# Output chunks in shared double buffers and the first keys in two transfers, in a top-32 attention with two MLPs

## The chip, the cores and the metric

The kernel runs on one core of a Trainium2 chip. The metric is the device time of one execution in microseconds (us). A core has five engines that run side by side and wait for each other by semaphores: TensorE (PE, matmuls; PEld is its weight load), VectorE (DVE), ScalarE (ACT), GpSimd (POOL) and SyncE (SP, which here only issues DMA transfers). Each engine takes its instructions strictly in order, so an instruction that waits holds up everything behind it on its engine. ACT also issues DMAs here: those of the output.

## The reference

Attention keeps the 32 largest scores of each row; then two MLPs follow, on 2304 tokens with model width 512 and hidden width 2048.

```python
scores = scale * np.matmul(q, k.transpose(0, 1, 3, 2))          # 4 batches, 8 heads, 576 x 576, head width 64
kth = np.partition(scores, -top_k, axis=-1)[..., -top_k:-top_k + 1]   # top_k = 32
scores = np.where(scores >= kth, scores, -1000000000.0)
attn = softmax(scores)                                          # written out in the reference
x = (attn @ v) reordered to [2304, 512]
h = np.maximum(x @ w_in, 0.0);   x = h * h @ w_out              # first MLP
h = x @ w_in2;   out = np.maximum(0.01 * h, h) @ w_out2         # second MLP
```

## The kernel before

**Tiling.** Tokens are cut into units (`UNITS`: a batch, a first row, 64 to 320 rows), and each unit has four head pairs. A unit and head pair gives score tiles of 128 rows; two tiles make a pair, and 72 pairs run one after the other through the whole attention. For each pair DVE finds the 32 largest of each row in four rounds of MAX8 (L867) with MATCH_REPLACE8 between them (L869). ACT turns the scores into exponentials (L321, L325), PE transposes them (L339, L354) and multiplies them with the values (L425 for the first two units, L436 later). The scores themselves are PE matmuls (L303) that ACT copies out of PSUM (L304).

**Split numbers.** Products are made of a rounded high part and a low part. `load_k` (L228) fetches the keys of a head pair, both heads in one transfer into `kraw`; `split_k` makes the high part (L128 on ACT for the first two key loads, L130 on POOL later) and the low part (L265; on DVE for the first load, on POOL later). `load_q` (L272) and `split_q` (L282) do the same for queries. For the first unit (256 rows, two heads) the first pair of tiles needs head 0 alone, the second pair head 1.

**MLPs.** When the tokens of a block (`BLOCKS`: 512, 256, 384, 512, 256, 384) are ready, generator `moe` runs its two layers, 16 steps of the hidden width each: matmuls into `h` (L619), ACT's `ga` and `gh` (L629, L630; L636, L638 in the second layer), the low part `gl` (L639), and matmuls into the accumulators `acc` (L656 in layer 0, L658 in layer 1). In the first block each step also converts its weights from 64-bit to 32-bit pieces (`w_convert`: `wraw` in, working buffer `wc`, L532 to L553) and stores them; later blocks load them back (`w_load`).

**Output.** At the end of layer 1 a block has n/128 accumulators. For each, L674 copies 512 columns out of PSUM into `y`, and L676 sends it to DRAM from ACT's queue, in two pieces where a chunk spans two units. `y` is the first half of a tile of 1024 columns with the tag `wc`, of which there are two buffers (`WCB = 2`); these are the buffers of the weight conversion. So the third chunk of a block waits until the transfer of the first has landed.

**What sets the order.** Work is put into numbered slots (`at`): 16 slots to a pair. `z` is the slot of a unit's first scores; keys are asked for at `z - 62`, queries at `z - 70` where nothing earlier holds them back. Instructions are emitted slot by slot, and a scheduler then lays out each engine's queue by priority and by its own model of the times, so that a small edit can shift rows all along the queues.

Of the kernel before, what the change touches and what calls it, by code (L numbers as in the profile page):

```python
# [8 lines left out]
F = mybir.dt.float32  # L9
# [49 lines left out]
WCB = 2  # L59
# [27 lines left out]
def topk_attention_moe_moe2_kernel(  # L87
# [12 lines left out]
    P = 128  # L100
# [8 lines left out]
    PE, ACT, DVE, POOL, SP = nc.tensor, nc.scalar, nc.vector, nc.gpsimd, nc.sync  # L109

    const = ctx.enter_context(tc.tile_pool(name="const", bufs=1))
    pool = ctx.enter_context(tc.tile_pool(name="work", bufs=2))
# [27 lines left out]
    for u in units:  # L140
        for hp in range(NHP):
            n = u["n"]
            uh = dict(u=u, hp=hp, n=n, b=u["b"], first=(u["t0"] == 0), i0=u["i"], ti=len(tiles), idx=len(uhs),
                      c0=P * (hp % 2) if n == 64 else 0)
# [14 lines left out]
    def direct(uh):  # L159
        return uh["b"] not in EARLY  # L160

    def kept(uh):
        return uh["u"]["i"] == KEPT

    def score_slot(ti):
        return 16 * (ti // 2) - DLEAD + 5 * (ti % 2)
# [10 lines left out]
    def split(uh):  # L177
        return uh["u"]["i"] >= NATIVE
# [36 lines left out]
    def at(slot, fn, *a):  # L215
        events.setdefault(slot, []).append((fn, a))
# [4 lines left out]
    def load_k(b, hp, st):  # L221
        if b in EARLY:
            KT[b, hp] = ahead.tile([P, 2, S], R, tag="KTa", name="KTa", bufs=KPB)
        else:
            KT[b, hp] = pool.tile([P, 2, S], R, tag="KT", name="KT", bufs=4)
        x = ahead if b in EARLY else pool
        st["k"] = x.tile([P, 2, S], F, tag="kraw", name="kraw", bufs=1 if b in EARLY else KRB)
        SP.dma_start(st["k"], k[b, hp])  # L228

    VT = {}  # L230
    vdram = {}
# [349 lines left out]
    def rows(g0, n):  # L581

        got = []
        for u in units:
            a, e = max(g0, u["g0"]), min(g0 + n, u["g0"] + u["n"])
            if a < e:
                got.append((a - g0, e - a, u["b"] * S + u["t0"] + a - u["g0"]))
        return got

    def moe(j, layer):  # L590
# [6 lines left out]
        for f in range(NF + LAG):  # L597
            conv = iter(())
            if f < NF:
# [24 lines left out]
                h = two.pop(0)  # L624
# [41 lines left out]
        for c in range(na):  # L666
            if layer == 0:
                xh, xl = x[c]
                with tc.high_priority(offset=SEAM):
                    ACT.activation(xh[:, 0:n], acc[c][:, 0:n], AF.Copy)  # L670
                    DVE.tensor_tensor(xl[:, 0:n], acc[c][:, 0:n], xh.bitcast(F)[:, 0:n], op=OP.subtract)
            else:
                y = pool.tile([P, 1024], F, tag="wc", name="y", bufs=WCB)[:, 0:512]
                ACT.activation(y, acc[c], AF.Copy)  # L674
                for p0, n0, r0 in rows(blk["g0"] + c * P, P):
                    ACT.dma_start(out[r0:r0 + n0, :], y[p0:p0 + n0])  # L676
# [9 lines left out]
    def after(z, *keys):  # L686
        return max([z] + [used[k] + 1 for k in keys if k in used])

    order = []
    for uh in in_time + [uh for uh in uhs if not direct(uh)]:  # L690
        b, hp, i = uh["b"], uh["hp"], uh.get("di")
        z = uh["zs"]
        if uh["first"] and direct(uh):
            st = {"i": i}
            st["n"] = len(order)
            order.append(b)
            z0 = after(z - 62, ("kraw", st["n"] - KRB), *[("KT", x, hp) for x in range(b)])
            at(z0, load_k, b, hp, st)
            for h in range(2):
                at(z0 + 12 * h + 11, split_k, b, hp, st, h)  # L700
            used["kraw", st["n"]] = z0 + 23
            assert z0 + 24 <= z
        if (b, hp) not in vdone or split(uh) and VTB < NHP:
            vdone.add((b, hp))
            zv = score_slot(uh["ti"]) + DLEAD + 4
            if split(uh):
                zv = max(zv, opened)
            at(zv, load_v, uh)
            if split(uh):
                at(zv + 6, split_v, uh, 0)  # L710
                at(zv + 9, split_v, uh, 1)
        if not direct(uh):
            continue
        uh["qs"] = qsets[i % 2]
        z0 = after(z - 70, ("qraw", i - 2))
        z1 = max(after(z - 20, ("q", i - 2)), z0 + 6)
        assert z1 + 4 <= z
        at(z0, load_q, uh)
        at(z1, split_q, uh, 0)
        at(z1 + 4, split_q, uh, 1)  # L720
        used["qraw", i] = z1 + 4
        used["q", i] = used["KT", b, hp] = (z if kept(uh) else score_slot(uh["last"])) + 2
# [129 lines left out]
    while slot <= last:  # L852
        p, i = divmod(slot, 16)
# [89 lines left out]
```

## Time and profile before

| What | us |
|---|---|
| Median of three runs (1192.93, 1192.21, 1192.61) | 1192.61 |
| The profiled execution: its own time | 1189.77 |
| Its span, from the first to the last instruction | 1188.0 |
| Busy in it: PE | 1124.0 |
| DVE | 872.1 |
| ACT | 820.1 |
| POOL | 744.8 |

The profile is of one execution, whose time is 2.84 us below the median; 1.77 us of it lie outside the span. Busy time of an engine says which engine has the least room over the whole span, and not which one sets the end in a given stage: for that the busy time in short stretches is read, then what an engine waited for there, then the chain of work that ended last. The granted clock (PEclk) is a share of TensorE's full rate: 1.00 is 2.4 GHz and 0.50 is 1.2 GHz.

### The profile page before, as it was taken

The numbers are of one execution on the slowest core, as the hardware profiler recorded it, in microseconds if no ns is written. First come the engines' busy times: TensorE is split into PE (matmuls) and PEld (weight loads), VectorE is DVE, ScalarE is ACT, GpSimd is POOL, SyncE is SP. The second block draws the span as 40 slices with busy tenths as digits, with TensorE's granted clock in tenths as the row PEclk, the third lists the DMA queues.
The fourth block names the chain that finished last, engine by engine and source line by source line (L and its number), as shares of the span: only waits on it lengthen the run. The fifth ranks groups of instructions, "written<-read, shape, count | busy, mean of one in ns | idle before, by whom it ended". The sixth has DMA issues, their size and how long they took to land.

```text
span 1188.0 us, 20096 instructions
## 1 busy us (share of the span) xinstructions
PE 1124.0 (95%) x6376; PEld 985.5 (83%) x6376; DVE 872.1 (73%) x1828; ACT 820.1 (69%) x1823; POOL 744.8 (63%) x958
## 2 busy tenths in 40 slices
PE   5899977989899999999999999999999999999997
PEld 4777765868688899898998998788888899998996
DVE  7999999888886668999999999989997400110010
ACT  6999998899989667887676777556766743332322
POOL 7968846999879677677886775767665653002100
PEclk9999989999899999999999999999999999999999
DMA  9868756899999698799888888667776499779973
GB/s 307 287 216 276 264 187 230 312 334 333 394 353 360 199 336 293 240 346 371 312 264 296 286 283 287 217 219 219 232 234 215 151 326 334 256 252 351 346 258 119
DMA packets 108201, 329.53 MB, mean 277 GB/s; under 512 B 17216, under 2 KB 25408, under 8 KB 104000
## 3 DMA queue, kind: packets, MB, share of 16 engines
q1 hardware_dynamic: 105472, 323.53, 79.8%
q10 hardware_dynamic: 2624, 4.72, 1.1%
q8 instruction: 52, 0.85, 0.3%
q14 instruction: 53, 0.43, 0.1%
HBM read 257.03 MB, written 71.17 MB: 276 GB/s over the span
## 4 chain that ended last, share of the span: by engine, by line
PE 57%; DVE 21%; ACT 12%; DMA 5%; issue 2%; POOL 2%; ACTq 0%; SPq 0%; POOLq 0%; DVEq 0%
PE h L619 22%; PE acc L658 13%; DVE m L867 10%; PE acc L656 9%; DVE w L869 8%; PE att L425 3%; PE att L436 3%; PE att L339 3%; ACT e L321 2%; ACT stage L304 1%; PE sp L303 1%; ACT e L325 1%; DMA wraw<-in_w_dram 1%; DMA out_dram<-y 1%; ACT s L304 1%
## 5 line engine op out<-in xcount | busy, mean ns | idle before, releaser
L619 PE MATMUL h<-xh,wi 128*128 128x512 f32 (+2 forms) x1280 | 345.9, 344 | 9.7 <-ACT ga L629 4.5
L867 DVE MAX8 m<-w 128x8 f32<-128x576 f32 x432 | 315.1, 756 | 1.8
L619 PEld LDWEIGHTS h<-xh,wi 128*128 128x128 f32 x1280 | 225.4, 190 | 38.6 <-ACT ga L629 6.7
L639 POOL TENSOR_TENSOR gl<-ga,gh 128x512 fp32r<-128x512 f32 (+2 forms) x160 | 162.5, 1018 | 137.2 <-ACT gh L638 110.9
L869 DVE MATCH_REPLACE8 w<-m,w 128x576 f32<-128x576 f32 x288 | 215.2, 751 | 0.5
L619 PE MATMUL h<-xl,wi 128*128 128x512 f32 (+2 forms) x640 | 203.3, 338 | 0.0
L347 POOL TENSOR_TENSOR PTs<-whole,PTs 128x512 fp32r<-128x512 f32 x112 | 144.6, 1297 | 43.7 <-ACT whole L346 43.2
L656 PE MATMUL acc<-gh,wo 128*128 128x512 f32 (+2 forms) x768 | 156.5, 343 | 0.8 <-ACT y L674 0.5
L658 PE MATMUL acc<-wo,gh 128*128 128x512 f32 x576 | 152.1, 396 | 0.5 <-ACT gh L638 0.5
L656 PEld LDWEIGHTS acc<-gh,wo 128*128 128x128 f32 x768 | 127.4, 190 | 13.4 <-ACT y L674 0.7
L321 ACT ACTIVATE e<-s,m 128x576 f32<-128x576 f32 x144 | 112.9, 785 | 32.3 <-DVE m L867 27.4
L639 DVE TENSOR_TENSOR gl<-ga,gh 128x384 fp32r<-128x384 f32 x32 | 17.9, 559 | 152.1 <-ACT gh L638 149.4
L619 PEld LDWEIGHTS h<-xl,wi 128*128 128x128 f32 x640 | 120.0, 189 | 10.6
L636 ACT ACTIVATE ga<-h 128x512 f32<-128x512 f32 (+2 forms) x96 | 46.6, 491 | 116.3 <-PE h L619 114.8
L658 PEld LDWEIGHTS acc<-wo,gh 128*128 128x128 f32 x576 | 105.4, 188 | 21.2 <-ACT gh L638 0.9
L867 DVE MAX8 m<-s 128x8 f32<-128x576 f32 x144 | 104.3, 754 | 17.7 <-ACT s L304 15.2
L325 ACT ACTIVATE e<-e,nb 128x576 f32<-128x576 f32 x144 | 111.5, 782 | 1.8 <-POOL nb L315 1.7
L869 DVE MATCH_REPLACE8 w<-m,s 128x576 f32<-128x576 f32 x144 | 108.2, 752 | 0.6
L339 PE MATMUL att<-ident,e 128*128 128x128 f32 x576 | 90.1, 277 | 7.6 <-DVE wc L548 3.0
L334 POOL TENSOR_SCALAR e<-e,rc 128x576 f32<-128x576 f32 x112 | 82.5, 748 | 16.0 <-DVE rc L330 14.5
L656 PE MATMUL acc<-gl,wo 128*128 128x512 f32 (+2 forms) x384 | 88.3, 349 | 3.8 <-POOL gl L639 3.8
L631 POOL TENSOR_TENSOR ga<-ga 128x512 f32<-128x512 f32 (+2 forms) x80 | 66.3, 829 | 36.9 <-ACT gh L630 36.7
(90 smaller groups left out, 2117.4 us busy)
## 6 DMA issues: line engine op xcount, KB each, us to landing
wi<-wd SPq DMA_DIRECT2D x160, 512.0 KB, 5.1
wo<-wd SPq DMA_DIRECT2D x160, 512.0 KB, 5.0
wraw<-in_w_dram SPq DMA_DIRECT2D x32, 1024.0 KB, 7.9
sd<-stage SPq DMA_DIRECT2D x76, 288.0 KB, 3.3
s<-sd SPq DMA_DIRECT2D x76, 288.0 KB, 4.8
wd<-wi SPq DMA_DIRECT2D x32, 512.0 KB, 7.8
wd<-wo SPq DMA_DIRECT2D x32, 512.0 KB, 8.4
vd<-VT SPq DMA_DIRECT2D x16, 640.0 KB, 5.8
```

The costliest lines, as they stand in the source:

```text
L321: ACT.activation(t["e"], t["s"], AF.Prelu, bias=pr["m8"][:, i, 31:32], scale=-1.0, alpha=1.0 / FAR)
L325: ACT.activation(e, e, AF.Exp, bias=pr["nb"][:, i:i + 1], scale=-FAR, accum_out=pr["sum"][:, i:i + 1])
L334: POOL.tensor_scalar(e, e, pr["rc"][:, i:i + 1], 1.0, op0=OP.mult, op1=OP.mult)
L339: PE.transpose(ps[:, j * P:(j + 1) * P], t["e"][:, j * P:(j + 1) * P], ident)
L347: POOL.tensor_tensor(pts[:, 4:8, c:c + P], whole, pts.bitcast(F)[:, 0:4, c:c + P], op=OP.subtract)
L619: PE.matmul(two[r][:, 0:n], lhsT=ws[r][:, w, c * P:(c + 1) * P], rhs=x[c][y][:, 0:n], start=cnt == mine[0], stop=cnt == mine[-1])
L631: POOL.tensor_tensor(a[:, 0:n], a[:, 0:n], a[:, 0:n], op=OP.mult)
L639: (DVE if j >= GLD else POOL).tensor_tensor(gl[:, 0:n], a[:, 0:n], gh.bitcast(F)[:, 0:n], op=OP.subtract)
L656: PE.matmul(acc[c][:, 0:n], lhsT=wo[:, w, cs], rhs=g[:, 0:n], start=first, stop=last)
L658: PE.matmul(acc[c], lhsT=g[:, cs], rhs=wo[:, w, :], start=first, stop=last)
L867: cur["dve"] = DVE.max(out=m8[:, x, 8 * r:8 * r + 8], in_=t["s"] if r == 0 else t["w"])
L869: cur["dve"] = DVE.match_replace(out=t["w"], in_to_replace=m8[:, x, 8 * r:8 * r + 8], in_values=t["s"] if r == 0 else t["w"], imm_value=NEG)
```

## The change

Three edits. The first key load is cut into two transfers, one for each head. The first query load is put twelve slots later, which is behind the first key load. And two output chunks share one tile of the tag `wc`, each in a half of it, so that two buffers hold four chunks.

```diff
-        SP.dma_start(st["k"], k[b, hp])
+        for h in range(2) if st["i"] == 0 else (slice(0, 2),):
+            SP.dma_start(st["k"][:, h], k[b, hp][:, h])
...
-                y = pool.tile([P, 1024], F, tag="wc", name="y", bufs=WCB)[:, 0:512]
+                if c % 2 == 0:
+                    y2 = pool.tile([P, 2, 512], F, tag="wc", name="y", bufs=WCB)
+                y = y2[:, c % 2]
                 ACT.activation(y, acc[c], AF.Copy)
...
-        at(z0, load_q, uh)
+        at(z0 if i else z0 + 12, load_q, uh)
```

Lines behind the first edit move down by one and those behind the second by three. No engine gains or loses a computing instruction; SP gets one more transfer. But the rows of every queue are laid out anew.

SP's queue at the start of the program, before and after (128x1152 is both heads of the keys, 128x576 one head):

```order
L272 DMA qraw<-in_q_dram 128x2x256
L228 DMA kraw<-in_k_dram 128x1152
L272 DMA qraw<-in_q_dram 128x2x256 x2
L272 DMA qraw<-in_q_dram 128x2x320
L228 DMA kraw<-in_k_dram 128x1152
```

```order
L229 DMA kraw<-in_k_dram 128x576
L273 DMA qraw<-in_q_dram 128x2x256 x2
L229 DMA kraw<-in_k_dram 128x576
L273 DMA qraw<-in_q_dram 128x2x256
L273 DMA qraw<-in_q_dram 128x2x320
```

The keys of head 0 go first, then the queries of two units, then the keys of head 1.

ACT's queue at the same place, up to the first scores (`s_101` is the first tile's; `sd` is the PSUM bank in which PE made them):

```order
L128 ACTIVATE q_77<-qraw 128x256 [waits DMAHW0_49]
L128 ACTIVATE q_77<-qraw 128x256
L128 ACTIVATE KT<-kraw 128x576 [waits DMAHW1_49]
L128 ACTIVATE KT<-kraw 128x576
L128 ACTIVATE q_83<-qraw 128x256 [waits DMAHW2_49]
L128 ACTIVATE q_83<-qraw 128x256
L304 ACTIVATE s_101<-sd 128x288 [waits PE_49] x2
```

```order
L128 ACTIVATE KT<-kraw 128x576 [waits DMAHW0_49]
L128 ACTIVATE q_77<-qraw 128x256 [waits DMAHW1_49]
L128 ACTIVATE q_77<-qraw 128x256
L128 ACTIVATE q_83<-qraw 128x256 [waits DMAHW2_49]
L128 ACTIVATE q_83<-qraw 128x256
L128 ACTIVATE KT<-kraw 128x576 [waits DMAHW3_49]
L305 ACTIVATE s_101<-sd 128x288 [waits PE_49] x2
```

The two high parts of the keys stood together; now the second one, which waits for its own transfer (DMAHW3), stands right ahead of the first scores.

ACT's queue at the end of the third block's layer 1 (three chunks; `ga` is the next block's first step):

```order
L674 ACTIVATE y_9339<-acc_8382 128x512 [waits PE_49]
L674 ACTIVATE y_9343<-acc_8383 128x512 [waits PE_49]
L676 DMA out_0_dram<-y_9339 64x512 [waits DMAHW1_49,Activation_49]
L457 ACTIVATE xh1_7368<-xf_9170 128x256 [waits DVE_49]
L676 DMA out_0_dram<-y_9339 64x512 [waits DMAHW2_49]
L363 ACTIVATE PTs_2609<-att_9440 64x256 [waits PE_49]
L676 DMA out_0_dram<-y_9343 128x512 [waits DMAHW3_49,Activation_49]
L321 ACTIVATE e0_107<-s0_101,m8_9499 128x576 [waits DMAHW6_49,DVE_49]
L674 ACTIVATE y_9346<-acc_8384 128x512 [waits DMAHW2_49,DMAHW1_49]
L676 DMA out_0_dram<-y_9346 128x512 [waits DMAHW5_49,Activation_49]
L629 ACTIVATE ga_9396<-h_9353 128x512 [waits PE_49]
L629 ACTIVATE ga_9417<-h_9354 128x512 [waits PE_49]
```

```order
L677 ACTIVATE y_9343<-acc_8382 128x512 [waits PE_49]
L458 ACTIVATE xh1_7366<-xf_9168 128x256 [waits DVE_49]
L679 DMA out_0_dram<-y_9337 64x512 [waits DMAHW2_49,Activation_49]
L679 DMA out_0_dram<-y_9337 64x512 [waits DMAHW3_49]
L679 DMA out_0_dram<-y_9337 128x512 [waits DMAHW4_49,Activation_49]
L679 DMA out_0_dram<-y_9343 128x512 [waits DMAHW5_49,Activation_49]
L364 ACTIVATE PTs_2610<-att_9437 64x256 [waits PE_49]
L322 ACTIVATE e0_107<-s0_101,m8_9496 128x576 [waits DMAHW7_49,DVE_49]
L345 ACTIVATE PTs_2610<-att_9548 128x4x128 [waits PE_49]
L347 ACTIVATE whole_9554<-att_9548 128x512 [waits Pool_49]
L345 ACTIVATE PTs_2610<-att_9576 128x4x128 [waits PE_49]
L347 ACTIVATE whole_9582<-att_9576 128x512 [waits Pool_49]
```

The third copy waits for PE alone and stands with the two others (of which it is the last), but the four copies of transposed exponentials (L345, L347) now stand ahead of `ga`, which follows them; they stood behind it.

ACT's queue at the end of the program:

```order
L674 ACTIVATE y_13969<-acc_13508 128x512 [waits DMAHW6_49,PE_49]
L674 ACTIVATE y_13973<-acc_13509 128x512 [waits DMAHW7_49,PE_49]
L676 DMA out_0_dram<-y_13969 64x512 [waits DMAHW0_49,Activation_49]
L676 DMA out_0_dram<-y_13969 64x512 [waits DMAHW1_49]
L676 DMA out_0_dram<-y_13973 128x512 [waits DMAHW2_49,Activation_49]
L674 ACTIVATE y_13976<-acc_13510 128x512 [waits DMAHW1_49,DMAHW0_49,PE_49]
L676 DMA out_0_dram<-y_13976 128x512 [waits DMAHW3_49,Activation_49]
```

```order
L677 ACTIVATE y_13963<-acc_13502 128x512 [waits DMAHW5_49,PE_49]
L677 ACTIVATE y_13963<-acc_13503 128x512 [waits PE_49]
L677 ACTIVATE y_13969<-acc_13504 128x512 [waits DMAHW7_49,DMAHW0_49,PE_49]
L679 DMA out_0_dram<-y_13963 64x512 [waits DMAHW1_49,Activation_49]
L679 DMA out_0_dram<-y_13963 64x512 [waits DMAHW2_49]
L679 DMA out_0_dram<-y_13963 128x512 [waits DMAHW3_49,Activation_49]
L679 DMA out_0_dram<-y_13969 128x512 [waits DMAHW4_49,Activation_49]
```

The third copy waited for the two transfers of the first chunk (DMAHW0 and DMAHW1, issued two and three rows above it); now it stands ahead of all four transfers, and the two that it names were issued at the end of the block before.

## Rows read from the trace of the kernel before

**Rows 1.** The page: busy time of TensorE; the last chain's shares by line.

```profile
PE 1124.0 (95%) x6376; PEld 985.5 (83%) x6376; DVE 872.1 (73%) x1828; ACT 820.1 (69%) x1823; POOL 744.8 (63%) x958
PE h L619 22%; PE acc L658 13%; DVE m L867 10%; PE acc L656 9%; DVE w L869 8%; PE att L425 3%; PE att L436 3%; PE att L339 3%; ACT e L321 2%; ACT stage L304 1%; PE sp L303 1%; ACT e L325 1%; DMA wraw<-in_w_dram 1%; DMA out_dram<-y 1%; ACT s L304 1%
```

**Rows 2.** The timeline, 0 to 10 us: start, length, engine, line, count, wait.

```profile
0.74 0.66 SPq L272 DMA_DIRECT2D qraw<-in_q_dram  x1
1.45 0.58 SPq L228 DMA_DIRECT2D kraw<-in_k_dram  x1
...
3.91 0.72 ACT L128 ACTIVATE q<-qraw 128x256 fp32r<-128x256 f32 x2 [1.89 <-DMA qraw<-in_q_dram]
...
4.35 0.76 DVE L282 TENSOR_TENSOR q<-qraw,q 128x256 fp32r<-128x256 f32 x2 [4.35 <-ACT q L128]
...
5.77 1.25 ACT L128 ACTIVATE KT<-kraw 128x576 fp32r<-128x576 f32 x2 [1.14 <-DMA kraw<-in_k_dram]
6.48 1.43 DVE L265 TENSOR_TENSOR KT<-kraw,KT 64x576 fp32r<-64x576 f32 x2 [1.37 <-ACT KT L128]
...
7.29 1.33 PE L303 MATMUL sd<-KT,q 128*128 128x288 f32 x4 [7.29 <-DVE KT L265]
7.80 0.78 POOL L130 TENSOR_SCALAR q<-qraw 128x256 fp32r<-128x256 f32 x2 [4.00 <-DMA qraw<-in_q_dram]
...
8.42 0.71 ACT L304 ACTIVATE s<-sd 128x288 f32<-128x288 f32 x2 [0.67 <-PE sd L303]
...
9.16 0.76 DVE L867 MAX8 m<-s 128x8 f32<-128x576 f32 x1 [1.25 <-ACT s L304]
```

**Rows 3.** DVE's waits from 10 to 210 us: total, times, longest.

```profile
DVE rc L330 <- POOL sum L329: 1.4, 3, 0.6
```

**Rows 4.** Stretches: length, busy PE, PEld, DVE, ACT, POOL; PEclk, DMA share, GB/s.

```profile
202.00:204.00 2.00, 0.00 (x0) 0.00 (x0) 2.00 (x6) 2.00 (x4) 2.00 (x3) 0.97 0.66 213
208.00:210.00 2.00, 2.00 (x7) 1.36 (x6) 2.00 (x6) 2.00 (x5) 1.83 (x4) 0.50 0.88 324
300.00:310.00 10.00, 5.66 (x25) 4.46 (x24) 6.90 (x13) 9.26 (x19) 10.00 (x12) 0.81 1.03 373
750.00:780.00 30.00, 30.00 (x147) 24.72 (x146) 29.44 (x65) 18.71 (x40) 21.57 (x28) 1.00 0.72 234
```

**Rows 5.** Instructions on tile y: ACT's idle time before them, times.

```profile
  DMA out_dram<-y: 8.5, 5
```

**Rows 6.** The timeline at the first block's end: ACT, then PE.

```profile
422.35 0.60 ACT L674 ACTIVATE y<-acc 128x512 f32<-128x512 f32 x1 [1.41 <-DMA out_dram<-y]
...
424.85 0.51 PE L656 MATMUL acc<-gh,wo 128*128 128x256 f32 x2 [0.54 <-ACT y L674]
```

**Rows 7.** The timeline at the third block's end: ACT (four rows), then PE.

```profile
729.03 1.07 ACT L674 ACTIVATE y<-acc 128x512 f32<-128x512 f32 x2
...
734.93 0.60 ACT L674 ACTIVATE y<-acc 128x512 f32<-128x512 f32 x1 [2.48 <-DMA out_dram<-y]
...
735.94 1.09 ACT L629 ACTIVATE ga<-h 128x512 f32<-128x512 f32 x2 [0.41 <-ACT y L674]
736.91 0.60 ACT L344 ACTIVATE PTs<-att 128x512 fp32r<-128x512 f32 x1
...
736.59 0.50 PE L619 MATMUL h<-xh,wi 128*128 128x512 f32 x1 [1.58 <-ACT ga L629]
...
743.91 1.20 PE L656 MATMUL acc<-gl,wo 128*128 128x512 f32 x4 [1.06 <-POOL gl L639]
```

**Rows 8.** The timeline at the program's end: PE, then ACT and its DMA issues.

```profile
1180.09 0.86 PE L658 MATMUL acc<-wo,gl 128*128 128x512 f32 x3
...
1180.51 1.08 ACT L674 ACTIVATE y<-acc 128x512 f32<-128x512 f32 x2 [2.69 <-PE acc L658]
1181.14 1.77 ACTq L676 DMA_DIRECT2D out_dram<-y  x3
1184.24 0.60 ACT L674 ACTIVATE y<-acc 128x512 f32<-128x512 f32 x1 [2.64 <-DMA out_dram<-y]
```

## The prediction

> **What bounds the kernel now.** I read the page first: PE is busy for 1124.0 us of the span of 1188.0, DVE for 872.1 [rows 1]. The last chain runs through PE lines for most of its length, through DVE's MAX8 and MATCH_REPLACE for about a fifth, and a small share of it, 1%, is the output's transfers themselves [rows 1]. Since stages differ, I then read stretches, and DVE's own waits. From 10 to 210 us DVE waited for next to nothing: the largest sum in its list of waits is 1.4 us, over three times [rows 3]. So there the attention goes at DVE's pace, and what comes before DVE's first MAX8 is paid in full. Around 300 us POOL is busy for all of its 10 us and PE for only 5.66 of them [rows 4]: there the first block's weight conversions and the attention's copies hold each other up. From the third block's end on PE is full (30.00 of 30 us in the stretch from 750 to 780 [rows 4]), so a wait of PE that goes away there is time off the end. At the end the output's transfers set the time alone. The change touches three of these places: what precedes DVE's first MAX8, the ends of blocks, and the end of the program.
>
> **The start.** Before, the first MAX8 starts at 9.16 us [rows 2]. In front of it stand the queries (issued at 0.74, there by 3.91), both heads' keys (issued at 1.45, there by 5.77), their high parts on ACT and low parts on DVE, four matmuls and two copies [rows 2]. The shapes give the sizes: queries of 256 rows and two heads are 256 KB, both heads' keys 576 KB. So 256 KB were there by 3.91, 832 KB by 5.77, and 1344 KB (two more query loads) by 7.80, where POOL's wait for the fourth transfer ends [rows 2]. That is 310 and 252 KB a microsecond. In the new order the sums at each landing are 288, 544, 800 and 1088 KB; between those points this gives about 4.0, 4.85, 5.7 and 6.8 us for head 0's keys, the first queries, the second queries and head 1's keys.
>
> Head 0's low part is then done by 4.0 + 0.71 + 0.81 = 5.5 us (the steps from 5.77 to 6.48 to 7.29), the queries by 4.85 + 0.44 + 0.76 = 6.05 (from 3.91 to 4.35, and DVE's two), and the four matmuls, which took 1.13 us from 7.29 to 8.42, by 7.2 [rows 2]. But the new order puts the high part of head 1's keys ahead of the first scores' copies on ACT, and its low part ahead of the first MAX8 on DVE. Behind it waits the whole of DVE. Head 1 lands at 6.8; ACT is done with it at 7.43 (half of 1.25) and with the two copies at 8.14 (0.71); DVE has the low part at 6.8 + 0.71 + 0.72 = 8.23. So the first MAX8 starts at about 8.2, which is 0.95 us earlier. Bounds: were head 1 no obstacle, the matmuls would decide, 7.2 + 0.74 = 7.95 (from 8.42 to 9.16), a gain of 1.2; if head 1 is as late as the fourth transfer was, 7.80, nothing is gained. I take 0.95 and carry it whole, because DVE's order behind it has no gap to lose it in until 210 us [rows 3] and the first block's MLP begins when the attention hands it its tokens; in the stage around 300 us it may be lost.
>
> **The ends of blocks.** ACT sat for 8.5 us, in five pieces, until an output transfer had landed [rows 5]. Three of them are 1.41, 2.48 and 2.64 us [rows 6 to 8]; the two others share the 1.97 that are left. All five go, since in the new order no copy of a block waits for a transfer of the same block. What that is worth is what PE waited for it.
>
> At the first block's end PE waited 0.54 us for the accumulators [rows 6]. That goes. But four copies and four issues now stand closer together, and `ga` of the next block, which stood between the second copy and the third, stands behind all four; PE's next matmuls into `h` need it. The nearest price of a late link there is the 1.06 us at the third block's end [rows 7]. I take 0, between a loss of 1.0 and a gain of 0.54.
>
> At the third block's end the third copy began 2.48 us late, and PE then waited 1.58 us for `ga` and 1.06 us for `gl` [rows 7]: 2.64 us if all of it goes. But the new order moves four copies of exponentials ahead of `ga`. They take about 0.5 us each (the first from 736.91, behind `ga`'s row that began at 735.94 and holds two [rows 7]), so about 1.9 of the 2.48 us are given back and `ga` comes some 0.55 us earlier. Beside that PE has the next attention product ahead of the matmuls that need `ga`, as filler. I take 1.0, between 0 and 2.64.
>
> **The end of the program.** PE's last matmuls end at 1180.09 + 0.86 = 1180.95, and the third copy started at 1184.24, when the first chunk had landed [rows 8]. Now it can start behind the two others, at 1180.51 + 1.08 = 1181.6. The three issues that took 1.77 us from 1181.14 [rows 8] now stand behind it, so they end at about 1183.4, and the last issue begins then and not at 1184.24 + 0.60 = 1184.84: 1.45 us earlier. From that issue to the end of the span were 1188.0 - 1184.84 = 3.16 us. If the last chunk now queues behind the other 512 KB, it loses up to 1.0 us (256 KB at 252 KB a microsecond); if the issues hide behind the copies, all of 1184.24 - 1181.6 = 2.65 is gained. I take 1.45, between 0.45 and 2.65.
>
> **The sum.** 0.95 + 0 + 1.0 + 1.45 = 3.4 us. The profiled execution would go from 1189.77 to 1186.4; the median, 2.84 us above it, from 1192.61 to 1189.2. The ends of the terms give gains from 0 - 1.0 + 0 + 0.45 = -0.55 to 1.2 + 0.54 + 2.64 + 2.65 = 7.0, which is 1193.2 to 1185.6.
>
> **The rivals.** *Only the end pays.* The start's gain is lost where DVE no longer leads, and `ga` is late at both block ends by other copies. For it speaks that POOL had no idle time at all around 300 us [rows 4], and that the new order puts work ahead of `ga` both times; against it, that the whole first stage moves with DVE. Then 1.45 us are left: 1191.2.
>
> *Transfers cost by the piece.* Each new transfer could delay those behind it as a whole one would, whatever its size. Head 1, now the fourth, would be there at 7.80 as the fourth was, and the start gains nothing: 3.4 - 0.95 = 2.45, so 1190.2. Against it speaks that the second transfer, of 576 KB, landed 1.86 us behind the first and the next two, of 256 KB each, 2.03 us behind that together [rows 2]: bytes, not pieces, fit both. The Trainium skill ("DMA: Bandwidth & Descriptors", Anatomy of one DMA) gives each DMA a fixed cost of about 2.0 us beside its bytes, which it measured on GpSimd's path and lays to the wait for completion; paid one behind the other it would put head 1 at some 8.8 us and make the start a loss of about 1.0 us. By that rule the sum would be 1.45 us, so 1191.2; two transfers that landed within 2.03 us [rows 2] speak for overlap.
>
> *One more stall of PE where the conversions run.* PE's queue is in order and has three PSUM banks for scores and transposes, which ACT's copies free. In the new order a weight conversion that waits for its transfer stands ahead of the copy of a second half of scores that it followed before, at the stage around 300 us. It decides from the point at which that transfer is later than the copy would have been. Its price is the stretch from 300 to 310 us once more: 10 - 5.66 = 4.34 us without matmuls, and a granted clock of 0.81, which is 3.8 us at half rate [rows 4]. At half rate 7 matmuls started in 2 us, at full rate 147 in 30, so 9.8 [rows 4]; the loss is 0.29 of 3.8, that is 1.1 us. The stretch from 202 to 204 us has no matmul at all, and at 208 the clock is 0.50 [rows 4], so a stall does bring the slow clock. With 5.4 us lost the time is 1194.6, or 1195.6 if the start's gain is waited away with it: slower than before.
>
> *The stall of that stage shrinks.* The same reshuffle may as well halve the 4.34 us, and all 2.64 us may go at the third block's end: 3.4 + 2.2 + 1.6 = 7.2, so 1185.4.
>
> That the change does not do what it says I leave out: each head's high part waits for its own transfer, and the second copy into a shared tile waits for PE alone.
>
> **How the numbers follow.** Chances: my sum 0.50, only the end 0.23, by the piece 0.08, one more stall 0.11, a smaller stall 0.08. A measurement of this kernel can tell about 0.2%, which is 2.4 us, from no change. Faster by more than that (under 1190.2) are most of my sum's own range, 0.42, the smaller stall, and half of the second rival: 0.54. Within it: 0.08 + 0.23 + 0.04 = 0.35. Slower: 0.11. The range goes from 1185.4, the lower end of my own terms, to 1194.6, where the stall begins to count; what is left out is most of the stall and the odd lower end, some 0.13.
>
> **What would show it.** Right: the first MAX8 at about 8.2 us and not 9.16; no idle time of ACT before `y` that a transfer ended; the last block's third copy within 1 us of the end of PE's last matmul (before, 1184.24 - 1180.95 = 3.3 us), and the span's end about 1.5 us nearer to it. The step on the block ends is right if PE's waits for `ga` and `gl` at the third block's end sum to about 1.6 us, and wrong if they are 0 or over 2.6. The carry is wrong if PE's busy time between 300 and 320 us falls, or if the first block's output comes later although the first MAX8 came earlier. The forecast as a whole fails if queues that the edits do not touch, POOL's and ACT's in the conversions, differ more than the three places do.

## The result: 14 us slower

| | us |
|---|---|
| After, median of four runs (1203.60, 1205.56, 1207.26, 1207.16) | 1206.36 |
| Before, beside them on the same chip | 1192.41 |
| Ratio, with its 95% interval | 1.0115 [1.0095, 1.0135] |
| The profiled execution after: its own time, its span | 1203.60, 1201.7 |

The forecast was 1189.2 us, in a range from 1185.4 to 1194.6. No engine has noticeably more to do; PE's busy time grew by 6.6 us and its idle time by 7.1. The page of the changed kernel, busy time:

```profile
PE 1130.6 (94%) x6376; PEld 989.6 (82%) x6376; DVE 873.6 (73%) x1828; ACT 818.8 (68%) x1823; POOL 746.9 (62%) x958
```

At two of the three places the waits for transfers went as told; what that was worth at the ends of blocks is another matter, and stands further below. ACT's instructions on tile `y` in the changed kernel, its idle time before them; the 8.5 us that ended with a transfer [rows 5] are gone:

```profile
L677 ACT ACTIVATE y<-acc x18: 575/599/638, 425.2 to 1196.6; 128x512 f32<-128x512 f32 x18
its engine sat idle before it (us, times) until:
  PE acc L659: 3.6, 2
  PE h L620: 0.4, 1
```

The timeline at the end of the program: the third copy starts 0.54 us after PE's last matmul (1195.20 + 0.86), and from the first copy to the end of the span it is 1201.7 - 1195.63 = 6.1 us, before 1188.0 - 1180.51 = 7.5 [rows 8]:

```profile
1195.20 0.86 PE L659 MATMUL acc<-wo,gl 128*128 128x512 f32 x3
1195.63 1.08 ACT L677 ACTIVATE y<-acc 128x512 f32<-128x512 f32 x2 [2.68 <-PE acc L659]
1196.26 0.49 ACTq L679 DMA_DIRECT2D out_dram<-y  x1
1196.60 0.60 ACT L677 ACTIVATE y<-acc 128x512 f32<-128x512 f32 x1
1196.79 1.74 ACTq L679 DMA_DIRECT2D out_dram<-y  x3
```

The third place, the start, gave 0.18 us in these two traces and not 0.95, and that is not clear of noise: in eight traces with the old order of the start the first MAX8 comes at 8.91 to 9.53 us, in six with the new one at 8.91 to 9.62. The timeline from 0 to 10 us (start, length, engine, line, wait), cut to the chain that leads to DVE's first MAX8:

```profile
3.66 0.68 ACT L128 ACTIVATE KT<-kraw 128x576 fp32r<-128x576 f32 x1 [1.65 <-DMA kraw<-in_k_dram]
...
5.03 0.72 ACT L128 ACTIVATE q<-qraw 128x256 fp32r<-128x256 f32 x2 [0.69 <-DMA qraw<-in_q_dram]
...
6.42 0.72 ACT L128 ACTIVATE q<-qraw 128x256 fp32r<-128x256 f32 x2 [0.67 <-DMA qraw<-in_q_dram]
...
7.37 0.68 ACT L128 ACTIVATE KT<-kraw 128x576 fp32r<-128x576 f32 x1 [0.22 <-DMA kraw<-in_k_dram]
7.96 0.69 ACT L305 ACTIVATE s<-sd 128x288 f32<-128x288 f32 x2
8.09 0.86 DVE L266 TENSOR_TENSOR KT<-kraw,KT 64x576 fp32r<-64x576 f32 x1 [1.84 <-ACT KT L128]
...
8.98 0.76 DVE L870 MAX8 m<-s 128x8 f32<-128x576 f32 x1
```

Where the 14 us lie is told by marks that every kernel has: the first MLP matmul, each block's first copy between its layers (a block's "seam"), its first output copy ("out"). The length of each stretch of the profiled execution before, and by how much others differ from it (us; the columns are runs of the sections below, `split_again` being the first keys in two transfers):

| Stretch up to | before | after | y_only | late_only | split_again | pair3_slot | split_y_last |
|---|---|---|---|---|---|---|---|
| first MLP matmul | 174.1 | +7.2 | +0.3 | +4.3 | +2.6 | +0.4 | +4.6 |
| seam 1 | 136.7 | +0.5 | -1.1 | -0.9 | -4.0 | +0.7 | -3.5 |
| out 1 | 104.8 | +2.0 | -0.2 | +1.6 | +0.7 | +0.1 | +1.7 |
| seam 2 | 70.3 | +3.9 | -2.1 | +0.6 | +3.9 | +4.7 | +1.9 |
| out 2 | 68.7 | +2.3 | +0.1 | +0.1 | -2.4 | -0.7 | -2.4 |
| seam 3 | 87.0 | -5.2 | +1.3 | 0.0 | -3.9 | -3.0 | -3.9 |
| out 3 | 87.5 | -0.4 | +2.2 | +0.2 | +3.9 | +10.1 | +3.8 |
| seam 4 | 110.1 | +1.5 | -1.5 | +1.8 | -4.8 | -2.3 | -4.8 |
| out 4 | 110.3 | +2.5 | 0.0 | +2.5 | 0.0 | +2.5 | 0.0 |
| seam 5 | 51.8 | +1.8 | -0.2 | -0.6 | +0.1 | +0.2 | 0.0 |
| out of the last block | 179.3 | -0.9 | -0.4 | -0.6 | -0.5 | -0.9 | -0.8 |
| end of the span | 7.5 | -1.4 | -1.3 | 0.0 | -0.1 | 0.0 | -1.4 |

In the column "after" only the last row is nothing but a place that the change was made for. The start is a small part of the first row, and the ends of blocks stand right behind each "out"; the rest of these stretches is work whose rows stand in another order. The largest difference, 7.2 us, arises before the first MLP matmul:

```profile
174.12 0.63 PE L619 MATMUL h<-xh,wi 128*128 128x512 f32 x1
```

```profile
181.32 2.03 PE L620 MATMUL h<-xh,wi 128*128 128x512 f32 x4
```

Each column is one execution. How far executions differ where the order does not is seen in kernels whose traces have the same rows up to a mark. With the order before, the first MLP matmul comes at 174.1, 174.4 (`y_only`), 175.5 (`pair5_slot`, but for four rows) and 176.2 us (`y_last_block`); at 176.7 to 178.7 in the three runs with only the first keys cut up to there (`split_only`, `split_again`, `split_y_last`); at 178.4 in `late_only` and 175.9 in `y_and_late`; at 181.3 in the changed kernel and 182.7 in `keys_only`. The stretch up to seam 2 took 72.2 to 75.7 us in the three with the cut keys. So an entry below some 2 us, at seam 2 below 3.5, tells nothing of the order; the 7.2 us are 5.1 to 8.6 us, by which traces are paired.

### The profile page after: what moved, and what is told of

Its sections match the earlier page's. It is cut to its first block, busy times and chain, and to the rows that moved or that the text cites. A ratio compares the mean times of both kernels' runs of the same rounds, so it can differ in the third digit from the quotient of the medians.

```text
span 1201.7 us, 20087 instructions
## 1 busy us (share of the span) xinstructions
PE 1130.6 (94%) x6376; PEld 989.6 (82%) x6376; DVE 873.6 (73%) x1828; ACT 818.8 (68%) x1823; POOL 746.9 (62%) x958
## 4 chain that ended last, share of the span: by engine, by line
PE 54%; DVE 5%; ACT 3%; DMA 2%; POOL 0%; issue 0%; ACTq 0%; DVEq 0%
PE h L620 24%; PE acc L659 12%; PE acc L657 11%; PE att L437 4%; PE att L340 3%; DVE m L870 2%; DVE w L872 2%; DMA wi<-wd 1%; PE att L355 1%; ACT e L326 1%; DMA vraw<-in_v_dram 0%; ACT whole L347 0%; ACT PTs L345 0%; PE att L304 0%; ACT e L322 0%
## 5 line engine op out<-in xcount | busy, mean ns | idle before, releaser
L620 PE MATMUL h<-xh,wi 128*128 128x512 f32 (+2 forms) x1280 | 349.4, 347 | 11.6 <-ACT ga L630 2.3
L620 PEld LDWEIGHTS h<-xh,wi 128*128 128x128 f32 x1280 | 228.2, 192 | 38.3 <-ACT ga L630 4.1
L340 PEld LDWEIGHTS att<-ident,e 128*128 128x128 f32 x576 | 69.3, 143 | 25.5 <-ACT e L326 10.5
```

What stands on the lines that cost most here:

```text
L340: PE.transpose(ps[:, j * P:(j + 1) * P], t["e"][:, j * P:(j + 1) * P], ident)
L620: PE.matmul(two[r][:, 0:n], lhsT=ws[r][:, w, c * P:(c + 1) * P], rhs=x[c][y][:, 0:n], start=cnt == mine[0], stop=cnt == mine[-1])
```

## Experiments

The theories. A: each edit makes the scheduler lay all queues out anew, and the new order is worth several us either way, whatever the edit is for. B: the shared buffers hold back what follows them. C: the cut and reordered first transfers are slower themselves. D: the edits cost by their place, the queries behind the keys above all. E, F and G, on the first MLP's start, stand with their runs. "Moved" counts rows of a queue that stand at another place than in the kernel before; PE's order has 6299 rows, which show as 6376 matmuls in a trace.

**The parts alone.** `y_only` is the change's second hunk (1831 of PE's rows moved, the first of them at the first block's end), `keys_only` the first and third (3622), `split_only` the first (3072), `late_only` the third (2574):

```diff
# y_only
+                if c % 2 == 0:
+                    y2 = pool.tile([P, 2, 512], F, tag="wc", name="y", bufs=WCB)
+                y = y2[:, c % 2]
# split_only, and keys_only
+        for h in range(2) if st["i"] == 0 else (slice(0, 2),):
+            SP.dma_start(st["k"][:, h], k[b, hp][:, h])
# late_only, and keys_only
+        at(z0 if i else z0 + 12, load_q, uh)
```

> Only the shared output buffers; both edits of the start are undone. Every queue reads as before up to the first block's end (some 415 us), so all three theories expect no lag there, within 0.5 us. Theory A (the loss is made by the relaid order of the first 300 us, and so by the edits of the start): 1191 to 1193 us, the end of the program about 1.4 us shorter after PE's last matmul, and at most a few us lost or won around 485 us. Theory B (the shared buffers hold back the conversions and the next block's first steps): at 1200 us or more, with the lag that the changed kernel gains at 430 and 485 us. Theory C (the first transfers themselves are slower): as before less 1.4 us, 1191.

> Both edits of the start; the output buffers are as before. Queues read as in the changed kernel up to some 415 us. Theory A: the lag of 8 to 9 us at 320 to 411 us is there as in the changed kernel; the total is 1200 to 1204 us, since only the 5 us of 485 us may be missing, and the end of the program is as long as before. Theory B: 1191.5 us, the small gain of the start alone, no lag at 320 us. Theory C: first MAX8 at 9.0 us, and a lag that is there already before 60 us.

> The first keys in two transfers, nothing else. The bytes and their order are as before, with one more issue. Theory A: the order of the queues is relaid from the start on, in another way than in the changed kernel, so that the time may go either way by several us, with the lag made between 100 and 320 us; the first MAX8 within 0.7 us of 9.16. Theory B: 1192.4, no change. Theory C: the more transfers, the later: first MAX8 at 9.8 us, and 1193.

> The first queries twelve slots later, so behind the first keys; keys in one transfer. Theory A: relaid in yet another way, several us either way, made between 100 and 320 us. Theory B: 1192.4, no change. Theory C: the keys come first and their rounding starts 1 us earlier, the queries land behind them: first MAX8 within 0.5 us of 9.16, and 1192.4.

| Run | median, us | ratio to before, 95% interval |
|---|---|---|
| y_only | 1189.2 | 0.9967 [0.9952, 0.9983] |
| keys_only | 1200.5 | 1.0068 [1.0043, 1.0092] |
| split_only | 1186.8 | 0.9954 [0.9937, 0.9971] |
| late_only | 1201.2 | 1.0075 [1.0049, 1.0102] |

B falls: the shared buffers alone gain 3.9 us, more than half of it before the end of the program. C falls: `late_only` has its first MAX8 at 8.78 us, earlier than before, and is slower; `split_only` has it at 9.40, later, and is faster. The three worths sum to -0.04%, and the change cost 1.15%.

**Two parts together, and edits that change no work.** `y_and_split` and `y_and_late` join two hunks. `pair3_slot` and `pair5_slot` put the transposes of one pair of tiles one slot later:

```diff
-            at(max(z + 20 + 3 * i, z + 21 + i), pt_main, t)
+            at(max(z + 20 + 3 * i, z + 21 + i) + (p == 3), pt_main, t)
```

> Shared output buffers and the first keys in two transfers; the first queries ahead of the keys, as before. If an edit's worth adds up, 1192.0 - 2.8 - 5.2 = 1184. Theory A (each edit lays the queues out anew, and most of what it is worth comes from that): the two do not add; anything from 1181 to 1195 us, of which only about 1.5 us at the end of the program belongs to the buffers for certain. Theory D (the first queries behind the keys are what costs, by their place): no loss here, 1184 us.

> Shared output buffers and the first queries behind the keys; keys in one transfer. If edits add up, 1192.0 - 2.8 + 9.2 = 1198.4. Theory A: the two do not add, as in the changed kernel, where the shared buffers came out some 6 us dearer than without the start's edits; 1193 to 1208 us. Theory D: 1198 us.

> The kernel before, with the transposes of the fourth pair of tiles (p == 3) put one slot of 16 later, some 1 us of a stage in which PE has room. No work, no transfer, no buffer differs; but the order of PE's queue differs in 3751 of 6299 rows from there on. Theory A: the time moves by several us, either way, and the lag is made in the stages where it was made in the other kernels (100 to 320 us and the layer seams). Theory D (it takes the edits' own costs to move the time): 1192 us, within 1 us.

> The same edit at the sixth pair (p == 5). Here the queues keep their order but for four rows of PE and two of ACT. Theories A and D: 1192 us, within 1 us. If it moves by more, a few rows in another place are enough, and the number of moved rows is no measure.

| Run | PE's rows moved | median, us | ratio to before, 95% interval | if worths added up |
|---|---|---|---|---|
| y_and_split | 3793 | 1195.7 | 1.0033 [1.0020, 1.0047] | 0.992 |
| y_and_late | 3989 | 1193.3 | 1.0015 [1.0003, 1.0028] | 1.004 |
| pair3_slot | 3751 | 1200.8 | 1.0081 [1.0050, 1.0112] | |
| pair5_slot | 4 | 1191.3 | 1.0004 [0.9990, 1.0019] | |

Two gains together are a loss, 13 us from their sum. And the slot of one pair's transposes, with no change of work, transfers or buffers, costs 0.8% where it moves 3751 rows of PE's queue; the same edit where it moves four rows costs nothing. A stands. The shared buffers and the cut keys change sign with what stands beside them. The late queries don't: they cost 9 us alone, 6 with the shared buffers (1.0015 against 0.9967), 14 with the cut keys, 10 with both. By their place at the start they cost nothing, since `late_only` has its MAX8 still 0.5 us ahead at 49 us; it is 4.3 us behind by 108, but `y_and_late`, with the same rows up to there, only 1.9, and `y_last_block`, with the order before, 1.8. Whether the scheduler's orders behind late queries are worse as a rule, or four times by chance, four pairs don't tell; D is left open in that form.

What such a loss looks like: behind the third block's seam, in the stretch of `pair3_slot` that is 10.1 us longer. The first `ga` comes there 11.9 us behind the seam and not 6.2, so some 5.7 of the 10.1 us arise at this place. ACT's timeline there, first of `pair3_slot`, then of the kernel before. The exponential `e`, which waits for DVE, now stands ahead of `ga`; before, `ga` came first:

```profile
654.15 0.77 ACT L321 ACTIVATE e<-s,m 128x576 f32<-128x576 f32 x1 [2.72 <-DVE m L867]
...
655.59 0.85 ACT L636 ACTIVATE ga<-h 128x384 f32<-128x384 f32 x2
```

```profile
647.70 0.87 ACT L636 ACTIVATE ga<-h 128x384 f32<-128x384 f32 x2 [1.77 <-PE h L619]
649.95 0.78 ACT L321 ACTIVATE e<-s,m 128x576 f32<-128x576 f32 x1 [1.38 <-DVE m L867]
```

PE's timeline of `pair3_slot`: its next matmul waits 2.80 us for `ga`, and the matmuls behind take 0.52 us each, where the kernel before took 0.33 to 0.34 (below):

```profile
652.28 1.03 PE L339 MATMUL att<-ident,e 128*128 128x128 f32 x8
656.11 0.45 PE L619 MATMUL h<-xh,wi 128*128 128x384 f32 x1 [2.80 <-ACT ga L636]
...
657.62 0.52 PE L619 MATMUL h<-xl,wi 128*128 128x384 f32 x1
```

```profile
649.51 0.34 PE L619 MATMUL h<-xh,wi 128*128 128x384 f32 x1
```

Stretches of that place (length, busy PE, PEld, DVE, ACT, POOL; PEclk, DMA share, GB/s): first `pair3_slot`, where PE is busy for 0.31 of 3 us and the granted clock of the next 3 us is 0.57, so that most of them ran at the lower of the two levels, 1.2 GHz; below it the kernel before at its own seam:

```profile
653.00:656.00 3.00, 0.31 (x3) 0.07 (x1) 3.00 (x7) 1.85 (x5) 0.20 (x1) 1.00 0.91 285
656.00:659.00 3.00, 2.89 (x10) 2.89 (x11) 3.00 (x7) 2.95 (x8) 0.40 (x2) 0.57 0.62 236
```

```profile
647.00:650.00 3.00, 2.93 (x20) 2.49 (x19) 3.00 (x8) 0.93 (x3) 1.40 (x3) 1.00 0.72 176
650.00:653.00 3.00, 2.46 (x14) 1.96 (x13) 3.00 (x6) 3.00 (x7) 1.22 (x3) 1.00 1.01 361
```

The changed kernel has the same ahead of its second block's seam (+3.9 us), where PE waits 1.99 us for ACT's copy `whole`:

```profile
497.00:500.00 3.00, 1.01 (x9) 0.78 (x8) 3.00 (x9) 2.95 (x10) 1.43 (x3) 1.00 0.48 123
500.00:503.00 3.00, 2.93 (x16) 2.62 (x14) 3.00 (x7) 2.55 (x8) 2.34 (x3) 0.59 0.16 57
```

**The first conversion four slots earlier**, in the kernel before, in the changed one and in `y_only`; and a no-work edit in the changed kernel. Theory E: the first MLP's start decides the time, and the conversions are what it waits for.

```diff
-    at(rslot[0] - 28, convert_now, 0)
+    at(rslot[0] - 32, convert_now, 0)
```

`after_pair13_slot` is the edit of `pair3_slot` at `p == 13`, in the changed kernel.

> The kernel before, with the first weight conversion put four slots earlier (32 instead of 28 slots ahead of the first block). Same work, same transfers; 2443 of PE's 6299 rows stand elsewhere, all from row 742 on, so nothing before some 150 us. Theory A (a relaid order is worth several us either way): 1183 to 1204 us, sign open. Theory E (the first MLP's start decides, and the conversions are what it waits for): the first MLP matmul comes before 174.1 us and the time falls by what it gains, 1187 to 1191.

> The changed kernel with the same edit, conversions four slots earlier; 3241 of PE's rows move against the changed kernel, from row 708 on. The start, the transfers and the buffers are those of the changed kernel. Theory A: anything from 1186 to 1212 us; the end of the program stays short (6.1 us from the last block's first output copy to the end of the span, 7.5 before). Theory D (the change's transfers or buffers cost by themselves): 1203 us or more. Theory E: the first MLP matmul comes some 3 us before 181.3, and the total falls by as much, to 1203.

> Shared output buffers alone, with the same edit. Theory A: 1182 to 1202 us, and no fixed relation to what the edit does to the kernel before; 6.2 us at the end. Theory E: as in the kernel before, the same gain, so about 1187.

> The changed kernel with the transposes of the fourteenth pair (p == 13) one slot later: no work differs, 3223 of PE's rows move, from row 656 on. Theory A: 1186 to 1212 us; the lag of the first 150 us is that of the changed kernel, what follows is open. Theory D: 1206 us, within 2.

| Run | first MLP matmul | median, us | ratio to before, 95% interval |
|---|---|---|---|
| conv_early | 172.5 | 1194.2 | 1.0014 [0.9996, 1.0032] |
| after_conv_early | 182.1 | 1195.5 | 1.0023 [1.0005, 1.0041] |
| y_conv_early | 173.7 | 1198.5 | 1.0052 [1.0034, 1.0071] |
| after_pair13_slot | 182.2 | 1195.8 | 1.0031 [1.0010, 1.0051] |

The same edit adds 2 us to the kernel before (its interval reaches down to no change), takes 11 from the changed one and adds 10 to `y_only`. E falls twice: `conv_early` starts its MLP 1.6 us earlier, which is inside the spread of one order, and reaches seam 1 only at 317.9 instead of 310.8; `after_conv_early` starts at 182.1, no earlier than the changed kernel, and yet regains most of the loss. `after_pair13_slot` regains as much with no work changed: the start's edits, the transfers and the buffers are all still in it, and some 10 of the 14 us are gone. The two are one witness and not two: by their traces all but 62 of PE's 6376 matmuls stand at the same places, and the 62 lie between 158 and 198 us. Two different edits led to nearly one order, and it has one time, 1195.5 and 1195.8 us; that speaks for A more plainly than its forecasts, which were up to 26 us wide and which two runs missed (`y_only` lies 2 us under its 1191, `y_and_split` 0.7 over its 1195). What stays is the late first MLP, in each of these kernels with both edits of the start (181.3 to 182.7 us).

**The scores made ahead.** ACT and PE also prepare the scores of later units in that stage (tile `sp`, 320 matmuls). Before, the last of them ran at 159.6 us; in the changed kernel at 178.6, right ahead of the first MLP matmul. Theory F: they stand in its way. Theory G: they only keep it company, and DVE's order of pairs or the conversions are the cause.

```diff
-FILL = (2, 245)
+FILL = (2, 210)
```

> The changed kernel with the scores that are made ahead (tile sp, 320 matmuls) spread over slots 2 to 210 instead of 2 to 245. In PE's queue the last of them then stands 51 rows ahead of the first MLP matmul; in the changed kernel 7 rows, in the kernel before 41. Theory F (the two edits of the start together let these scores fall behind, and they stand in front of the first MLP): the last sp matmul at about 165 us instead of 178.6, the first MLP matmul at 174 to 177 instead of 181.3, and some 5 us less in the total, if later stages don't take them back: 1190 to 1203. Theory G (the late first MLP comes from DVE's order of pairs or from the conversions alone, the sp rows only keep it company): first MLP matmul at 180 to 183.

> The same with slots 2 to 190: the last sp row stands 89 rows ahead of the first MLP matmul. Theory F: the last sp matmul at about 155 us, and the first MLP matmul at 172 to 177, no much earlier than with 210, since then the attention's own products are what it waits for. Theory G: 180 to 183.

> The reverse: the kernel before, with these scores spread over slots 2 to 265, nothing else. The last sp row stands 13 rows ahead of the first MLP matmul instead of 41. Theory F: last sp matmul at 170 to 178 us instead of 159.6, and the first MLP matmul at 178 to 182 instead of 174.1, without any of the change's edits. Theory G: 174, within 1.5. Total by theory A anything from 1188 to 1206.

| Run | last `sp` | first MLP matmul | median, us | ratio to before, 95% interval |
|---|---|---|---|---|
| after_fill210 | 165.6 | 182.6 | 1201.8 | 1.0079 [1.0051, 1.0106] |
| after_fill190 | 162.2 | 189.2 | 1219.6 | 1.0239 [1.0220, 1.0258] |
| before_fill265 | 169.6 | 175.8 | 1190.6 | 0.9986 [0.9969, 1.0003] |

F falls: 13 us earlier out of the way, the MLP starts no earlier; 10 us later in the kernel before, it starts 1.7 us later, inside the 174.1 to 176.2 us of the order before. G's number, 180 to 183, holds for `after_fill210`, whose trace is of its fastest run (1195.7 us), and `before_fill265` lies 0.3 us outside of its 174 +- 1.5 and 2 us under F's. At 190 both miss, F's 172 to 177 and G's 180 to 183: there the attention itself falls behind (its 81st MAX8 comes at 125.3 us, in the changed kernel at 110.7), and the kernel is 1.2% slower than the changed one. Stretches from 0 to the first MLP matmul (columns as above), of the kernel before, the changed one, `after_fill210` and `after_fill190`, each from its own trace:

```profile
0.00:174.10 174.10, 144.93 (x820) 118.90 (x821) 165.22 (x355) 154.87 (x423) 129.05 (x214) 0.98 0.78 256
```

```profile
0.00:181.30 181.30, 147.06 (x818) 118.02 (x819) 171.60 (x368) 156.56 (x427) 130.83 (x216) 0.99 0.74 243
```

```profile
0.00:182.60 182.60, 149.43 (x817) 121.04 (x817) 166.14 (x354) 155.75 (x422) 129.40 (x215) 0.96 0.73 244
```

```profile
0.00:189.20 189.20, 153.25 (x818) 123.41 (x819) 164.50 (x351) 156.13 (x421) 129.96 (x214) 0.93 0.71 236
```

ACT is busy for 155 to 157 us in all four and idle for the rest: 19.2, 24.7, 26.9 and 33.1 us. Of the 7.2 us, 5.5 are then idle time of ACT and 1.7 work that now stands ahead. By itself this is arithmetic: an engine with the same work ahead of a later start has idled longer, and POOL's 129 to 131 us show it as well. What speaks for ACT is what it waited for, and that it got less done. From 40 to 160 us, before and in the changed kernel (columns as above), it was busy for 113.9 and 106.8 us, while DVE was about as full:

```profile
40.00:160.00 120.00, 110.17 (x666) 91.66 (x667) 118.13 (x258) 113.94 (x325) 93.98 (x143) 1.00 0.76 253
```

```profile
40.00:160.00 120.00, 106.35 (x620) 84.91 (x618) 117.08 (x253) 106.83 (x302) 90.93 (x139) 1.00 0.70 233
```

What ACT waited for in that time (total, times, longest), the kernel before and then the changed one:

```profile
ACT e L325 <- POOL nb L315: 1.7, 3, 0.9
ACT s L304 <- PE sd L303: 1.4, 2, 0.9
ACT e L321 <- DVE m L867: 1.3, 1, 1.3
```

```profile
ACT stage L305 <- PE sp L304: 5.4, 8, 0.9
ACT rb L391 <- PE att L376: 4.0, 5, 1.0
ACT e L326 <- POOL nb L316: 2.4, 3, 1.4
ACT e L322 <- DVE m L870: 1.7, 3, 1.1
```

In the new order ACT's copies `stage` and `rb` stand at places where PE has not made their inputs yet, 9.4 us that the old order did not have; `keys_only`, with the same rows, has 6.6 and 5.7, and `after_fill210` 5.3 and 3.6. That the order of these rows is the cause was not tried by a kernel that moves them alone; it is read from the waits, and a rival stands. DVE too is busier ahead of the changed kernel's first MLP matmul, 171.6 us and not 165.2, with 13 more instructions, and idles for only 0.8 us more: four more MAX8 run before that matmul. Whether these rows of DVE hold the MLP back, as G has it, or only run while it is late, no run tells; in `after_fill210` and `after_fill190` DVE has no such rows and idles for 16.5 and 24.7 us.

**The buffers in the last block alone.** There only four rows of ACT's queue change their place and none of any other engine.

```diff
+                if c % 2 == 0 or blk["idx"] + 1 < len(blocks):
+                    y2 = pool.tile([P, 2, 512], F, tag="wc", name="y", bufs=WCB)
+                y = y2[:, c % 2 if blk["idx"] + 1 == len(blocks) else 0]
```

> The kernel before, with the shared output buffers in the last block alone. In all queues only four rows change their place, the last three copies and issues of ACT's; nothing else is laid out anew. Theory A: the gain is what the end of the program gave in every kernel with shared buffers, 7.5 to 6.1 or 6.2 us from the last block's first output copy to the end of the span, so 1.3 us and no more, with no phase ahead of it off by over 1 us. If the shared buffers have a cost of their own elsewhere, it is not here, so this alone can't tell; but if the 1.3 us do not come, the gain was another thing's.

> The first keys in two transfers, with shared output buffers in the last block alone; against the split alone only four rows of ACT's queue move. Theory A: the two add up, since nothing else is laid out anew: 1.3 us below the split alone, so about 1185.5 us. With the shared buffers in all blocks the same two edits gave 1195.7.

> The first keys in two transfers, once more, beside the two others on the same chip. Theory A: an order that is laid out once stays what it is, so 1186.8 us again, within 1.5.

| Run | median, us | ratio to before, 95% interval | first output copy of the last block to the end |
|---|---|---|---|
| y_last_block | 1190.2 | 0.9981 [0.9970, 0.9992] | 6.2 |
| split_again | 1187.2 | 0.9947 [0.9935, 0.9960] | 7.4 |
| split_y_last | 1185.0 | 0.9930 [0.9917, 0.9944] | 6.1 |

Here the edits add up: 0.9981 x 0.9947 = 0.9928. That no stretch ahead of the end differs by over 1 us from the kernel before was expected for `y_last_block` and did not come: up to the first MLP matmul it took 2.1 us longer with the same rows, which is the spread of one order. `split_again` repeats `split_only` within 0.4 us, so an order that was laid out once keeps its worth. `split_y_last` is faster than both kernels, by 8.0 us than the one before. Of these, the split's 5 to 6 us come with the order that it happened to bring, since its first MAX8 is later than before; the 1.3 to 1.4 at the end are the buffers' own.

## Why the prediction was wrong

*The carry of the start* is a step that failed. "I carry it whole, because DVE's order behind it has no gap": DVE stayed as full as before up to 160 us (117.1 of 120 us, before 118.1), and the first MLP matmul still came 7.2 us later. A full DVE queue did not carry the start to the MLP: what stands ahead of the MLP in the queues had changed. The prediction read DVE's waits there and not ACT's, where the waits grew; that ACT's pace is the cause is the likeliest reading and not shown. One of the prediction's two signs for a wrong carry came: the first output is later (425.2, before 415.6) behind an earlier first MAX8. The other did not: PE's busy time from 300 to 320 us rose, from 14.1 to 16.1 us, and the stretch up to seam 1, which holds that stage, is only 0.5 us longer. The stage that was watched was not the one that lost.

*The missing term* weighs more. It was told ahead of the prediction that every queue's rows are laid out anew; the sum prices only the three places and puts the rest at nothing. It appears as two rivals at the stage of 300 us, a stall (0.11) and a smaller stall (0.08). The stall had the right kind, PE idle and then a slow clock, but as one event at one place for 5.4 us. The runs show many, at the first MLP and at the seams, of either sign, and a no-work edit that is worth 9 us. With that as a term the range would have reached some 10 us to either side (an estimate from the 9 us of `pair3_slot`), and the 3.4 us of the sum could not have carried a chance of 0.54 for faster. The last sentence of the prediction's signs, queues that the edits do not touch differing more than the three places, is what happened. (A slip beside it: the range's 1185.4 is called the lower end of the sum's own terms, which is 1185.6; 1185.4 is the smaller stall's.)

*The start's size* failed as well. The chain was right: DVE's first MAX8 waits behind the low part of head 1. Its landing was put at 6.8 us and came at 7.37, and the low part took 0.86 and not 0.72 us; that is 0.7 of the 0.78 us between 8.2 and 8.98. The landings follow each other by 1.37, 1.39 and 0.95 us for 256, 256 and 288 KB: not the even rate by bytes that was assumed. The fixed 2.0 us of the Trainium skill ("DMA: Bandwidth & Descriptors", Anatomy of one DMA), paid one behind the other, do not fit them either: all three steps are shorter.

*The ends of blocks.* At the first, PE waited 0.38 us for `ga`, before 0.54 for the accumulators: the 0 was right. At the third, PE waited for neither `ga` nor `gl`, only 0.9 us for `PTs`; 1.6 us were expected to stay, and by the prediction's own sign a sum of 0 makes the step wrong. Whether this is a gain of 2.6 us can't be told from the moved rows around it.

*The end of the program* was put at 1.45 us and gave 1.4; in every kernel with shared buffers in the last block it was 1.3 to 1.4, in the others up to 0.1. The place was right, and the size is partly luck: two misses cancel. The first issue went out ahead of the third copy, so the last one began 2.06 us behind PE's end and not 3.93, 1.87 us earlier instead of 1.45; and its transfer, behind the three others, landed 2.57 us after it and not 2.01. The prediction had named both, as the bounds of this term.

## What to carry to other kernels

Where a scheduler lays out the queues by its own model of the times, first try an edit that changes no work: if it moves the time by 0.8%, as here, gains below that can't be forecast from the edit's own places, and they do not add up. Then count the rows that an edit moves, on engines that it does not touch too. The count tells that the time may move, not how far or which way: 1831 moved rows gained 0.3% here, 2574 lost 0.8% and 3072 gained 0.5%. Before a stretch of one trace is compared with that of another kernel, look how far it differs between two traces of one order. An edit that can be confined until it moves only its own rows, like the buffers in the last block, keeps the gain that its waits promise.

## What was not expected of the hardware

A gap in PE's work is paid twice, by the gap and by the clock behind it: in `pair3_slot` PE was busy for 0.31 of 3 us, and in the next 3 us the granted clock was 0.57, mostly the lower level of 1.2 GHz, and a 128x384 matmul took up to 0.52 us instead of 0.34. This agrees with the Trainium skill ("TensorE: Matmul & The Clock Gate", Part 1), which gives an idle array half of its full rate. In the changed kernel the same came at 497 us, with 1.01 us busy of 3 and then 0.59. Four transfers of 256 to 288 KB, issued from 0.74 to 2.52 us, landed 0.95 to 1.39 us apart, the last and larger one at the shortest distance.
